# A loop that deals out projections between sine and exponential stages: eleven spends a group with a share for each group, and u's first step placed by group

## The chip, the core and the metric

The kernel runs on one core of one Trainium2 chip. The metric is the device time of one execution in microseconds (us); lower is better. The names of the engines in the profile are PE (TensorE's matmuls), PEld (its weight loads), DVE (VectorE), ACT (ScalarE), POOL (GpSimd) and SP (the queue that issues most DMAs).

## The reference: what is computed

A gated mix of two blocks over one sequence x of 2048 rows and 448 columns (x is `A_u`):

```python
g = _sigmoid((x * gate_w).sum(-1, keepdims=True))
a = _A_ref(x, ...)   # K = 2 Re sum_n C exp(A dt l); y = causal convolution of x with K, by FFT; + x * D_skip
b = _B_ref(x, ...)   # q, k, v = x @ wq, wk, wv; 16 heads of 28; 4 segments of 512 rows:
                     #   causal softmax attention inside a segment, mixed with a memory
                     #   M, z of the segments before (phi(q) M / phi(q) z); then @ wo
return g * a + (1 - g) * b
```

## The kernel before, in words

The work has two halves. The **first half** (`first_half`, L316) computes the convolution kernel K and has the attention's projections dealt out between its steps. The **second half** (`second_half`, L1250) does the Fourier transforms of K and u, the attention, and the output. It starts with `transform_k`, which needs all of K, and with the first loads of q and k. This change touches the first half alone.

*The loop of the first half.* K is made in 56 steps (`n`, L475) of eight channels, four to a group, so 14 groups (`n // 4`). For a step, `turns` (PE) makes the angles of the *next* step, `trig` (L411, ACT) takes three activations for sine and cosine, `product` (L421, DVE, its four instructions at L428 to L436) multiplies them with the exponentials into X and Y, two buffers each, and `sums` (L438, PE) contracts X and Y of the step *before* over the states: 64 small matmuls into `ps_k`. Between two groups stand `decays(g)` (L459): the exponentials of the next group, one ER (`decay_x`, L353) and two EY (`decay_y`, L379). Each has a matmul, then an exponential on ACT; POOL turns them into EX and EH. Since the exponential and the sine are in different tables, ACT loads a table ahead of the decays and one behind them. Inside decays, `sums` of the last step of the group before stand behind the first EY.

*The projections.* `project` (L720) is a generator: it yields the estimated cost of what it has just issued, in us. For each of four segments s of 512 rows it transposes x (four steps of 1.0), makes v (`values`, four tiles of 128 rows, two steps of 1.2 each), and q and k in units (s, hg, m): four heads hg, m = 0 for q and 1 for k. A unit is twelve matmuls (`matmuls`, L782), three to a step of 0.65, with weights that `load_w` fetches from DRAM a unit ahead, into two buffers. The first steps split the weights into two parts each and store them to DRAM (`weights`, L751: eight steps of -0.3 and 0.6, with a copy on ACT, a subtraction on POOL at L766, and a store; their two buffers are those of `load_w`). Most units need an exponential too (phi). They go in pairs, and after a pair the generator yields `"pe"`: the projections are then *held*, with two of the three PSUM buffers `ps_m` in use, until ACT has the table of exponentials. The others (`plain`) need none. A pair that is through leaves its memory to be done (`remember`): for q a recall (1.0), for k a transposition (-1.1) and a memory product (0.6). A negative cost ends the spend that it is in.

*u's first step.* `transform_u` (L552) multiplies u with a Fourier matrix, in 32 halves (16 positions w, two halves each). A half is a load, a matmul into `ps_m`, a copy and a store to GU. With `k.pairs` it does both halves of a w in one step, otherwise one.

*What sets the order.* PE runs in program order. In the loop `k.strict` chains ACT's activations and copies in program order as well. The order is thus what the class `Feed` (L501) deals out: `spend` adds credit to `due` and takes steps of the projections while there is credit and they are not held; `exps` releases a hold just ahead of each of the three exponentials in decays; `rest` does what is left after the loop. In the kernel before, a spend follows each `trig` and each part of decays, seven in a group, `due` is capped at 4.0 and set to zero when a hold is released. u's step is reached in two ways: as a step inside `project` (13 places that yield `-next(filling, 0.1)`, in pairs) and one half at a time when more than 1.5 is due during a hold. With `k.exps` (the second and third spend of decays) copies go to DVE instead of ACT. `feed.fill` does halves of u near the end.

Of the kernel before, what the change touches and what calls it, by code (L numbers as in the profile page):

```python
# [315 lines left out]
def first_half(nc, k, gy, feed):  # L316
# [142 lines left out]
    def decays(g):  # L459
        for i, (f, J) in enumerate(((decay_x, 2 * g), (decay_y, 2 * g), (decay_y, 2 * g + 1))):  # L460
            f(J)
            if g > 0 and i == 1:
                sums(4 * g - 1)
            if g > 0:
                k.exps = i >= 1
                feed.spend(PLACE[i] * RATES[g])
                k.exps = False

    room = []
# [5 lines left out]
    for n in range(2 * NJ):  # L475
        if n < 4:
            load(n + 2)
        elif n % 2 == 0:
            load(n // 2 + 4)
        if n % 4 < 3:  # L480
            turns(n + 1)
        trig(n)
        feed.spend(1.87 * RATES[n // 4])
        product(n)
        if n == 2 * NJ - 1:
            feed.fill(2)
        if n % 4 > 0:
            sums(n - 1)
        if n % 4 == 3 and n + 1 < 2 * NJ:
            decays(n // 4 + 1)  # L490
            turns(n + 1)
# [1 line left out]
    sums(2 * NJ - 1)  # L493


PLACE = (1.24, 0.9, 0.9)

RATES = (1.65, 1.65, 1.24, 1.55, 1.55, 1.17, 1.17, 1.48, 1.55, 1.17, 1.17, 1.48, 1.48, 1.65)


class Feed:  # L501
# [5 lines left out]
    def __init__(self, k, steps, filling):  # L507
        self.k = k
        self.steps, self.held, self.done, self.due, self.count = steps, False, False, 0.0, 0
        self.filling, self.waiting, self.ends = filling, False, False  # L510

    def step(self):
        tag = next(self.steps, None)
# [3 lines left out]
        self.ends = cost < 0  # L517
        return abs(cost)

    def spend(self, us):  # L520
        self.due = min(self.due + us, 4.0)
        self.ends = False
        while self.due > 0 and not (self.held or self.done or self.ends and self.waiting):
            self.due -= self.step()
        if self.due > 1.5 and (self.held or self.done) and self.waiting:
            self.k.pairs = False
            self.due -= next(self.filling, 0.0)
            self.k.pairs = True

    def exps(self):  # L530
        if self.held:
            self.due = 0.0
            self.step()

    def until(self, n):
# [181 lines left out]

def project(nc, k, pp, early, filling):  # L720

    act, copy, v = k.act, k.copy, nc.vector
    gw = pp.tile([112, 4, 2], F32, name="gw")
# [161 lines left out]

    for s in range(NSEG):
        if s > 0:
            yield -next(filling, 0.1)
        xh = pp.tile([112, 4, SEG], F32R, tag="xh", name="xh")
        xl = pp.tile([112, 4, SEG], F32R, tag="xl", name="xl")  # L890
        for t in range(4):
            xin = pp.tile([128, D], F32, tag="xin", name="xin", bufs=4)
            with k.issue_after(holds[s]) if s in holds else ExitStack():
                nc.sync.dma_start(xin, k.u[SEG * s + 128 * t : SEG * s + 128 * t + 128])
            pt = k.ps("m")
            for kt in range(4):
                k.tr(
                    pt[:112, 128 * kt : 128 * kt + 128], xin[:, 112 * kt : 112 * kt + 112], k.ident
                )
            pv = pt[:112].rearrange("p (k q) -> p k q", k=4)  # L900
            ts_ = slice(128 * t, 128 * t + 128)
            copy(xh[:, :, ts_], pv, AF.Copy)
            v.tensor_tensor(xl[:, :, ts_], pv, xh[:, :, ts_], ALU.subtract)
            yield -1.0 if s == 0 or t % 2 else 1.0
        yield from remember()
        if s > 0:
            yield from values(s, xh, xl, range(1))
        if s == 0:
            split = weights()
            for _ in range(4):  # L910
                yield next(split)

        if s == 0:
            plain = [(s, h, 0) for h in range(4)]
            units = [(s, h, 1) for h in range(4)]
        elif s == 3:
            plain = [(s, h, 1) for h in range(4)]
            units = [(s, h, 0) for h in range(4)]
        else:
            plain = []  # L920
# [12 lines left out]
        if s == 0:  # L933
            yield from values(s, xh, xl, range(4))
            for x_ in split:
                yield -0.3
                k.turn_over(k.ps("m"), 3)
                yield 0.6
            yield from rest_of(plain)
        for i in range(0, len(units), 2):  # L940
            us = units[i : i + 2]
            pts = []
            light = i == 2 if s == 0 else i > 2 and s < 3
            if s > 0 and i == 2:
                yield from values(s, xh, xl, range(1, 4))
                store_v(s)
            for u in us:
                if pts:
                    for _ in range(1 if light else 0):
                        yield -next(filling, 0.1)  # L950
                    yield from remember()
                    for _ in range(1 if light else 0):
                        yield -next(filling, 0.1)
                pts.append((yield from matmuls(u, x)))
                load_w(after[u])
                yield 0.65
            yield "pe"
            es, his, phs = [], [], []
            for u, pt in zip(us, pts):
                es.append(raised(pt))  # L960
                his.append(high(u, pt))
            for u, pt, e, hi in zip(us, pts, es, his):
                phs.append(phi(pt, e))
                store(u, pt, hi)
            if s == 0 and i == 0:
                store_v(s)
            pending += zip(us, phs)
            yield 0.1
        if s == 3:
            yield from rest_of(plain)  # L970
# [399 lines left out]
def gated_mix(ctx, tc, k):  # L1370
    nc = tc.nc
# [17 lines left out]
        return tc.keep_in_program_order(nc.scalar.activation(*args, **kw))  # L1389

    k.exps = False
    k.pairs = True

    def copy(out, x, f, **kw):

# [144 lines left out]
    with ExitStack() as st:  # L1540
# [17 lines left out]
        pp = pool(st, "pp", "right")  # L1558
        tu = transform_u(nc, k, pool(st, "up", "right"))

        def work(proj):
            for i, tag in enumerate(proj):
                yield tag
                if i == 100:
                    more_constants()

        gy = pool(st, "gy", "right")
        with ExitStack() as s2:
            early, prm = pool(s2, "early"), pool(s2, "prm", "right")
            feed = Feed(k, work(project(nc, k, pp, prm, tu)), tu)  # L1570
            half = first_half(nc, k, gy, feed)
            load_decay, load_phase, decays, room = next(half)
            params = prepare_params(nc, k, prm, early, gp)
            n = next(params)
            k.ct = gp.tile([128, 2, 512], BF16, name="ct")
            constants()
            while n is not None:
# [10 lines left out]
                n = next(params, None)  # L1588
# [68 lines left out]
```

## Time and profile before

| | |
|---|---|
| runs of the kernel, us | 897.26, 907.48, 912.32 (median 907.48) |
| the profiled execution, us | 906.73 |
| its span in the trace, us | 904.3 |
| mean granted clock of TensorE | 0.92 |
| the loop's groups 0 to 13, us from the span's start | 66.6 to 424.6 |
| last sums end, first transform of K starts | 430.4, 476.4 |

The span runs from the first to the last instruction. Busy time of an engine counts its instructions, not its queue. Matmuls are pipelined, so the mean duration of one is longer than the distance from one to the next; the time of a block of matmuls is read from its first start to its last end. In the timeline and the chain the columns are start, duration, engine, line, what it writes and reads, how many, and in brackets the idle time before it with what ended it. In the busy time by stretches a row has the stretch, its length, the busy time of each engine, the mean granted clock, the share of the DMA engines and their rate.

### The profile page before, as it was taken

To read this page: it belongs to the slowest core of one execution; us is meant where nothing else is said; L and a number is where in the kernel's file an instruction comes from. 1 tells how busy PE (TensorE), PEld (TensorE's weight loads), DVE (VectorE), ACT (ScalarE), POOL (GpSimd) and SP (SyncE) were. 2 spreads that over 40 slices of the span, in tenths; PEclk is the share of its full clock that TensorE was granted. 3 is DMA by queue.
4 is the path that set the end of the run, shared out by engine and by line. 5 is a ranking of instruction groups with operands and counts; after the bars stand their busy time and mean duration, and the time that the engine had idled before them with its cause. 6 is when DMAs were issued, how large, how long until landed. Compare 5 with 4: busy or idle time off the path is not lost.

```text
span 904.3 us, 19003 instructions
## 1 busy us (share of the span) xinstructions
PE 761.0 (84%) x7549; PEld 418.0 (46%) x7549; DVE 609.0 (67%) x1151; ACT 501.5 (55%) x609; POOL 243.8 (27%) x301
## 2 busy tenths in 40 slices
PE   1686798888889788977987799989997999788997
PEld 1363455646446455644763344434443444334433
DVE  7888468778688878989425655656475646765564
ACT  4857477788878888787322135545354434342320
POOL 5234333034333333332000011132222122333110
PEclk9998899999889998998997759999999999988799
DMA  9236664133246312442377775665566465455773
GB/s 229 81 86 189 187 212 151 42 106 132 75 162 211 133 62 93 150 157 80 124 267 280 266 271 156 198 233 192 190 198 199 156 231 189 151 178 206 200 241 100
DMA packets 88290, 152.91 MB, mean 169 GB/s; under 512 B 20626, under 2 KB 57290, under 8 KB 88154
## 3 DMA queue, kind: packets, MB, share of 16 engines
q1 hardware_dynamic: 79130, 140.64, 48.1%
q10 hardware_dynamic: 7424, 9.18, 2.9%
q0 software_dynamic: 1648, 1.89, 0.7%
q8 instruction: 59, 0.97, 0.5%
q14 instruction: 29, 0.24, 0.1%
HBM read 90.67 MB, written 60.63 MB: 167 GB/s over the span
## 4 chain that ended last, share of the span: by engine, by line
PE 52%; DVE 16%; ACT 14%; DMA 8%; issue 6%; SPq 2%; POOL 1%; ACTq 0%; DVEq 0%; POOLq 0%
PE ps_a L1416 19%; PE ps_m L1416 18%; PE ps_pv L1416 7%; ACT cs L1380 7%; PE ps_arg L1416 4%; PE ps_k L1416 3%; DVE jk L1037 3%; DVE Y L434 2%; DVE X L428 1%; ACT L1380 1%; PE ps_m L1419 1%; DMA ku<-KD 1%; DMA w<-WD 1%; DMA WD<-wsp 1%; DVE Y L435 1%
## 5 line engine op out<-in xcount | busy, mean ns | idle before, releaser
L1037 DVE CUSTOM_DVE_ANT_0 jk<-ps_a,mk 128x512 f32<-128x512 f32 (+3 forms) x256 | 125.0, 488 | 54.5 <-PE ps_a L1416 47.2
L1068 ACT ACTIVATE PT<-ps_a 128x1024 f32<-128x1024 f32 (+1 forms) x96 | 84.5, 881 | 124.4 <-PE ps_a L1416 107.5
L1380 ACT ACTIVATE cs<-ps_arg 128x1024 f32<-128x1024 f32 x111 | 107.4, 1022 | 17.8 <-PE ps_arg L1416 15.7
L1416 PE MATMUL ps_m<-xh,w 112*128 112x512 f32 x256 | 91.6, 413 | 11.8 <-DMA w<-WD 10.3
L1416 PE MATMUL ps_k<-Y,X 128*32 128x64 f32 x3584 | 69.4, 235 | 32.7 <-DVE Y L435 31.0
L1079 POOL TENSOR_SCALAR_AFFINE_SELECT PT<-PT 128x256 f32<-128x256 f32 (+1 forms) x96 | 47.4, 496 | 181.1 <-ACT PT L1068 176.7
L1416 PE MATMUL ps_a<-qu,ku 32*128 32x512 f32 (+3 forms) x768 | 92.8, 363 | 1.3 <-DVE mx L1037 0.6
L376 POOL TENSOR_TENSOR EX<-ER,cab 128x512 f32<-128x512 f32 x28 | 29.9, 1089 | 217.7 <-ACT ER L1380 206.6
L1416 PEld LDWEIGHTS ps_k<-Y,X 128*32 128x32 f32 x3584 | 59.0, 119 | 58.9 <-DVE Y L435 44.8
L428 DVE TENSOR_TENSOR X<-EX,cs 128x1024 f32<-128x1024 f32 x56 | 71.4, 1275 | 18.9 <-ACT cs L1380 17.1
L434 DVE TENSOR_TENSOR Y<-EY,cs 128x1024 f32<-128x1024 f32 x56 | 72.5, 1294 | 0.0
L1416 PEld LDWEIGHTS ps_a<-qu,ku 32*128 32x128 f32 x768 | 64.6, 200 | 10.1 <-issue 3.2
L390 POOL TENSOR_TENSOR EH<-EY,ga 128x512 f32<-128x512 f32 x56 | 66.4, 1213 | 5.6 <-ACT EY L1389 4.9
L1416 PE MATMUL ps_a<-ku,qu 32*128 32x512 f32 (+3 forms) x256 | 48.6, 419 | 18.9 <-DMA ku<-KD 10.2
L1416 PEld LDWEIGHTS ps_m<-xh,w 112*128 112x128 f32 x256 | 49.0, 191 | 31.5 <-issue 15.7
L436 DVE SCALAR_TENSOR_TENSOR Y<-EH,cs 128x512 f32<-128x512 f32 x56 | 43.8, 783 | 28.0 <-ACT cs L1380 23.1
L1380 ACT ACTIVATE cs<-cs 128x1024 f32<-128x1024 f32 x56 | 59.3, 1059 | 1.8
L1416 PEld LDWEIGHTS ps_a<-ku,qu 32*128 32x128 f32 x256 | 23.7, 201 | 67.8 <-issue 34.3
L1416 PE MATMUL ps_arg<-ct,lh 64*128 64x512 bf16 x224 | 45.6, 409 | 7.7 <-ACT cs L1380 5.9
L1416 PE MATMUL ps_m<-xl,w 112*128 112x512 f32 x128 | 50.8, 397 | 0.0
L646 DVE TENSOR_TENSOR pr<-ps_a,ks 128x896 f32<-128x896 f32 x32 | 34.7, 1085 | 15.8 <-PE ps_a L1416 15.4
L1416 PE MATMUL ps_m<-wo,pvs 128*128 128x448 f32 x96 | 42.6, 590 | 1.6 <-ACT tb L1172 1.4
(221 smaller groups left out, 1437.0 us busy)
## 6 DMA issues: line engine op xcount, KB each, us to landing
w<-WD SPq DMA_DIRECT2D x32, 448.0 KB
qu<-QD SPq DMA_DIRECT2D x16, 512.0 KB
ku<-KD SPq DMA_DIRECT2D x16, 512.0 KB
GU<-gs SPq DMA_DIRECT2D x32, 224.0 KB
GK<-gs SPq DMA_DIRECT2D x8, 896.0 KB
gk<-GK SPq DMA_DIRECT2D x32, 224.0 KB
gu<-GU SPq DMA_DIRECT2D x32, 224.0 KB
BB<-bs ACTq DMA_DIRECT2D x16, 448.0 KB
```

What stands on the lines that cost most here:

```text
L376: nc.gpsimd.tensor_tensor(o[:, :, :, :16], r, over(k.cab, lo, hi, 16), ALU.mult)
L390: nc.gpsimd.tensor_tensor(EH[J, c].rearrange("p t (d l) -> p t d l", l=32), EY[J][:, c].rearrange("p t (d l) -> p t d l", l=32), over(k.ga ...
L428: v.tensor_tensor(X, ex, t[:, :, 0], ALU.mult)
L434: v.tensor_tensor(Y[:, :, :, :32], lo, y[:, :, :, ::-1], ALU.mult)
L435: v.tensor_tensor(Y[:, 0, :, 32:], hi, y[:, 0], ALU.mult)
L436: v.scalar_tensor_tensor(Y[:, 1, :, 32:], hi, -1.0, y[:, 1], ALU.mult, ALU.mult)
L646: nc.vector.tensor_tensor(pr[c], pt, ks.pop(c), ALU.mult)
L1037: v.tensor_tensor_reduce(junk[:, :n], pt[:, x, o : o + n], k.mk[:, SEG - n :], 1.0, -3e38, ALU.add, ALU.max, mx[:, 3 - t, h : h + 1],)
L1068: nc.scalar.activation(PT[:, 2 * hp : 2 * hp + 2, 512 * b : 512 * b + n], pt[:, :, :n], AF.Exp, scale=SCALE)
L1079: nc.gpsimd.affine_select(sl, sl, pat, ALU.is_ge, 0.0, base=0, channel_multiplier=-1)
L1380: x = op(*args, **kw)
L1416: tc.keep_in_program_order(nc.tensor.matmul(*args, **kw))
```

## The change

Four things, all in how work is dealt out; nothing that is computed changes.

1. A spend names its group and a slot. There are eleven in a group: three in decays (0.9, 0.7, 0.7) and two for each step, one behind `trig` and one behind `sums` (0.5 each). Each gives its part, slot / 6.3, of the group's share in `SHARES`.
2. `due` has no cap any more and isn't set to zero when a hold is released.
3. u's first step leaves `project` and the holds. Each group has a number in `FILLERS`, dealt out over the same slots; when a whole one has come together, both halves of a w are done, whether or not the projections are held. They sum to 13 of the 16 w; the last three are halves at the end (two, four, and two in `rest`).
4. `k.pairs` is false outside of that.

```diff
-                feed.spend(PLACE[i] * RATES[g])
+                feed.spend(g, PLACE[i])
...
         trig(n)
-        feed.spend(1.87 * RATES[n // 4])
+        feed.spend(n // 4, TRIG)
         product(n)
         if n == 2 * NJ - 1:
             feed.fill(2)
         if n % 4 > 0:
             sums(n - 1)
+        feed.spend(n // 4, TRIG)
...
-PLACE = (1.24, 0.9, 0.9)
-RATES = (1.65, 1.65, 1.24, 1.55, 1.55, 1.17, 1.17, 1.48, 1.55, 1.17, 1.17, 1.48, 1.48, 1.65)
+PLACE = (0.9, 0.7, 0.7)
+TRIG = 0.5
+SHARES = (12.4, 11.6, 8.9, 15.2, 15.3, 8.1, 8.1, 14.5, 15.3, 8.1, 8.1, 14.5, 14.6, 12.8)
+FILLERS = (1, 0, 2, 0, 0, 2, 3, 0, 0, 2, 3, 0, 0, 0)
+SLOTS = sum(PLACE) + 8 * TRIG
...
-    def spend(self, us):
-        self.due = min(self.due + us, 4.0)
+    def spend(self, g, share):
+        part = share / SLOTS
+        self.due += SHARES[g] * part
+        self.credit += FILLERS[g] * part
         self.ends = False
         while self.due > 0 and not (self.held or self.done or self.ends and self.waiting):
             self.due -= self.step()
-        if self.due > 1.5 and (self.held or self.done) and self.waiting:
+        if self.credit > 0.99:
+            self.credit -= 1.0
+            self.k.pairs = True
+            next(self.filling, None)
             self.k.pairs = False
-            self.due -= next(self.filling, 0.0)
-            self.k.pairs = True
 
     def exps(self):
         if self.held:
-            self.due = 0.0
             self.step()
...
-            yield -next(filling, 0.1)
+            yield -0.1
...
-                    for _ in range(1 if light else 0):
-                        yield -next(filling, 0.1)
                     yield from remember()
-                    for _ in range(1 if light else 0):
-                        yield -next(filling, 0.1)
```

More of the change, by code (lines that the diff above doesn't have):

```diff
@@ L509, in __init__ @@
         self.steps, self.held, self.done, self.due, self.count = steps, False, False, 0.0, 0
-        self.filling, self.waiting, self.ends = filling, False, False
+        self.filling, self.waiting, self.ends, self.credit = filling, False, False, 0.0
     def step(self):
@@ L716, in finish, with project @@
     return load, join, last
-def project(nc, k, pp, early, filling):
+def project(nc, k, pp, early):
     act, copy, v = k.act, k.copy, nc.vector
@@ L942, in project @@
             pts = []
-            light = i == 2 if s == 0 else i > 2 and s < 3
             if s > 0 and i == 2:
@@ L1391, in gated_mix @@
     k.exps = False
-    k.pairs = True
+    k.pairs = False
     def copy(out, x, f, **kw):
@@ L1569, in gated_mix @@
             early, prm = pool(s2, "early"), pool(s2, "prm", "right")
-            feed = Feed(k, work(project(nc, k, pp, prm, tu)), tu)
+            feed = Feed(k, work(project(nc, k, pp, prm)), tu)
             half = first_half(nc, k, gy, feed)
```

## The prediction

> **What bounds the kernel now.** I began with the totals of the page, then took the busy time by stretches, with the cuts at the loads of the exponential table on ScalarE, which open each group of the loop.
>
> ```profile
> span 904.3 us, 19003 instructions
> PE 761.0 (84%) x7549; PEld 418.0 (46%) x7549; DVE 609.0 (67%) x1151; ACT 501.5 (55%) x609; POOL 243.8 (27%) x301
> ```
>
> ```profile
> core 0: us, PE busy (x) PEld busy (x) DVE busy (x) ACT busy (x) POOL busy (x), PEclk, DMA share, GB/s
> 66.60:123.80 57.20, 42.49 (x607) 25.72 (x603) 37.23 (x39) 33.31 (x38) 20.54 (x17) 0.88 0.64 193
> 123.80:224.60 100.80, 86.81 (x1386) 54.48 (x1386) 78.30 (x100) 84.77 (x101) 35.60 (x32) 0.95 0.39 123
> 224.60:424.60 200.00, 169.52 (x2656) 104.35 (x2656) 163.93 (x208) 163.87 (x187) 70.46 (x64) 0.93 0.37 124
> 424.60:430.40 5.80, 3.83 (x129) 3.43 (x129) 5.80 (x10) 3.45 (x6) 0.52 (x1) 0.50 0.25 93
> 430.40:476.40 46.00, 41.31 (x190) 32.11 (x186) 15.52 (x29) 14.21 (x25) 1.60 (x1) 0.99 0.57 194
> ```
>
> The rows are groups 0 and 1, groups 2 to 5, groups 6 to 13, the last sums, and then 46.0 us in which PE is busy 41.31 and DVE and ACT 15: the projections that the loop left over. In the loop no engine is full: of the middle 100.80 us PE has 86.81, ACT 84.77, DVE 78.30. The chain of waits through the leftover runs on PE, and on loads of weights:
>
> ```profile
> 436.00 23.75 PE ps_m L1416 x108
> 459.77 3.48 DMA w<-WD
> 463.38 3.02 PE ps_m L1416 x12
> 466.42 5.14 DMA w<-WD
> 479.67 6.50 DMA ku<-KD
> ```
>
> 108 matmuls in 23.75 us are nine blocks of twelve at 2.64 us: that is a projection unit (q or k of four heads) or 128 rows of v. A quarter unit is 0.66.
>
> **The deal, worked out from the code.** Each step of the projections names a cost, and a spend takes steps until its credit is used. Adding these costs gives the order of both kernels. Before, the loop ends as (2,3,k) is held: all of segment 3 (32 quarter units, 8 half rows of v, the transposes, five recalls) is left. After, the shares use up everything but the gates and two halves of u. So the 46.0 us go, and their work must fit into the loop.
>
> The holds do not all fall where the shares mean them to. Groups 0 and 1 deal out 12.4 x 4/6.3 + 11.6 = 19.47. From the point where the parameters are done, the first hold is 21.8 away (weights 6.0, four plain units at 2.65, two held units at 2.6). The missing 2.3 are dealt in the three spends of decays(2), and the hold comes after that group's last exponential. So it stays until decays(3). The next two come late likewise, the uncapped due climbs to 13.2 at the end of group 3 and 13.4 at the end of group 4, and is worked off in two bursts: in group 4's second turn (memory, v rows, two units), and in decays(5), first spend (three blocks of v rows, a unit, a recall, a transpose). From group 6 on each hold falls in the decays as meant.
>
> **The parts and their prices.** The small steps, from PE's timeline:
>
> ```profile
> 131.13 0.91 PE L1416 MATMUL ps_m<-ut,s1u 64*128 64x448 f32 x2
> 430.37 2.03 PE L1419 MATMUL ps_m<-ident,xin 128*112 128x128 f32 x12
> 433.70 1.12 PE L1416 MATMUL ps_m<-ph,macc 128*128 128x512 f32 x2
> 434.67 0.60 PE L1419 MATMUL ps_m<-ident,ph 128*128 128x128 f32 x4
> 436.00 1.16 PE L1416 MATMUL ps_m<-v,pkT 128*128 128x128 f32 x8 [0.74 <-ACT pkT L1380]
> ```
>
> In that order: a half of u's step, three input transposes (0.68 each), a recall, a key transpose, a memory product.
>
> (1) The tail: -46.0. What comes in its place is two halves of u after the last sums, 2 x 0.91, and up to 2 us of waits for their copies. The four halves before the last sums lie beside DVE, which is busy for all of 424.60 to 430.40. I take +3 (ends +2 and +4). The load of ku (6.50) stands behind the last stores in SP's queue, before (AM, DM) as after (GU): no change.
>
> (2) Groups 0 and 1. Eight spends instead of four bring the last six weight splits forward, two a turn. The chain there now:
>
> ```profile
> 73.42 5.40 DMA WD<-wsp
> 82.96 1.71 POOL wsp L766
> 84.68 3.39 DMA WD<-wsp
> 89.83 3.22 DMA WD<-wsp
> 93.12 3.61 DMA w<-WD
> 96.87 4.62 PE ps_m L1416 x12
> ```
>
> There are two buffers, so a pair of splits costs about 1.7 on POOL and 3.2 to 5.4 for the store, and the third pair waits on ACT ahead of the turn after it. Pairs at 70, 78 and 84 us end the stores near 89.5, and the first unit starts near 93, not 96.87. But PE now meets it in turn 3, ahead of the sums and of decays(1), which were beside the wait before. From there two quarter units, the sums and decays of 9 to 11 us (8.9 in the rows of part 3) move trig 4 from 102.50 (its row is there too) to about 107. Group 1's four turns then carry 12 quarter units, not 20 (7.7 us of PE, where 13.2 were): about 15 us instead of 21.3. Sum -1; from -6 to +8, if either half alone holds.
>
> (3) Groups 2 to 5. What decays cost today, on ScalarE:
>
> ```profile
> 102.50 1.02 ACT L1380 ACTIVATE cs<-ps_arg 128x1024 f32<-128x1024 f32 x1 [11.04 <-PE ps_arg L1416]
> ...
> 276.15 1.28 ACT L1380 ACT_TABLE_LOAD   x1
> ...
> 282.68 1.02 ACT L1380 ACTIVATE EY<-ps_arg 128x1024 f32<-128x1024 f32 x1 [1.26 <-PE ps_arg L1416]
> 283.72 1.28 ACT L1380 ACT_TABLE_LOAD   x1
> 285.09 1.94 ACT L1380 ACTIVATE cs<-ps_arg 128x1024 f32<-128x1024 f32 x2
> ```
>
> That is 8.9 us, and each EY waits for its matmul, which stands behind the spend ahead of it on PE. In decays(5) that spend is now 4 x 2.64 + 1.12 + 0.60 = 12.3 us. Then come the sums, a memory product, a unit and a pair of u's halves while two of three PSUM buffers are held, so that its second half waits for a copy: 1.1 (the 64 sums, below) + 1.16 + 2.64 + 1.82 + 0.6 for the wait = 7.3. With the last EY (1.02), the table (1.28) and the waits around them decays(5) take about 24 us: +15. Group 4: the burst of 1.16 + 3 x 2.64 = 9.1 stands before the sums that free X and Y, of which there are two: about +5; its decays get the four input transposes that group 3 had, +4.5. Groups 2 and 3 have nearly idle turns: -1 and -4. Sum +19. At best the bursts pay for themselves in part beside DVE and ACT: +8; at worst the work added here, 10 us of PE, comes on top: +28.
>
> (4) Groups 6 to 13 take in 22 quarter units, 8 half rows of v, 4 transposes and 4 recalls more, and one memory product and 4 halves of u (with the two behind the last turn) fewer: 14.5 + 10.6 + 2.7 + 4.5 - 1.2 - 3.6 = 27 us of PE. What that costs, from groups 4 to 11:
>
> ```profile
> 177.80:200.20 22.40, 18.83 (x322) 10.35 (x322) 13.13 (x15) 19.14 (x22) 8.57 (x8) 0.92 0.31 96
> 200.20:224.50 24.30, 21.79 (x350) 14.86 (x350) 19.88 (x27) 21.66 (x26) 9.58 (x8) 1.00 0.40 138
> 224.50:248.00 23.50, 19.29 (x324) 11.04 (x324) 16.52 (x20) 19.21 (x23) 8.63 (x8) 0.85 0.23 72
> 248.00:276.10 28.10, 24.88 (x320) 13.91 (x324) 22.09 (x29) 21.28 (x25) 8.57 (x8) 0.88 0.46 148
> 276.10:299.10 23.00, 21.11 (x319) 12.55 (x307) 20.94 (x28) 21.31 (x26) 8.62 (x8) 1.00 0.66 217
> 299.10:328.70 29.60, 23.91 (x423) 16.45 (x424) 25.64 (x36) 22.21 (x27) 8.17 (x8) 0.94 0.28 93
> 328.70:350.90 22.20, 17.89 (x316) 9.79 (x316) 15.67 (x17) 19.12 (x21) 9.56 (x8) 0.85 0.23 77
> 350.90:375.00 24.10, 23.07 (x299) 16.29 (x300) 20.04 (x27) 21.32 (x26) 9.57 (x8) 1.00 0.37 132
> ```
>
> The three sparse groups (4, 6, 10) take 22.7 us with 18.7 of PE. The two that were dealt evenly (8, 11) take 23.55 with 22.1: 0.25 us for each us of work. All five dense ones take 25.8 with 22.95: 0.73. Smaller spends speak for the first; the waits that stay (transposes and memory products between PE and a copy) for the second. I take 0.5: +13.5; ends 0.25 (+7) and one for one (+27).
>
> (5) Queues. u's loads and stores on SP are as many as before, moved by some groups; a GU store holds SP until its copy, at most about 3 us, with a weight load behind it, and that load is a unit ahead. Without that cover it is 3.61. POOL's splits move ahead of EX and EH, which wait for ER anyway. Both at nothing.
>
> Sum: -46 + 3 - 1 + 19 + 13.5 = -11.5. The profiled execution took 906.73 us, so 895.2; the median of the three runs, 907.48, stands 0.75 above it: 896.
>
> **The rivals.** *The loop soaks it up.* At 0.25 in (4) and the lower end in (3): -46 + 3 - 1 + 8 + 7 = -29, 878 us. For it speak groups 8 and 11; against it, that the due is 13 when group 5 begins. Or my count to the first hold is wrong, the shares do what they say, and (3) is near zero: 877.
>
> *PE becomes the bound.* Every moved us of PE costs one, in groups 2 to 5 too: -46 + 3 - 1 + 29 + 27 = +12, 919 us, slower than now. Its place is every group from 4 on; with (3) at +19 it turns the sign once a us of work costs more than 0.93. For it: group 9, 29.60 us with 23.91 of PE. Against it: group 11, 24.10 with 23.07.
>
> *A denser loop runs at a higher clock.* The granted clock is 0.88 to 0.95 in the loop's rows and 0.99 in the tail, and one and the same set of 64 sums has taken
>
> ```profile
> 138.08 1.93 PE L1416 MATMUL ps_k<-Y,X 128*32 128x64 f32 x64 [2.52 <-DVE Y L435]
> ...
> 143.09 1.10 PE L1416 MATMUL ps_k<-Y,X 128*32 128x64 f32 x64
> ```
>
> At full clock PE's busy time in the three loop rows would shrink by 42.49 x 0.12 + 86.81 x 0.05 + 169.52 x 0.07 = 21 us at most; at 0.5 us for each, -10.5, 886 us. Against it: group 4 and 5 get long waits in which PE has nothing. By the Trainium skill (TensorE: Matmul & The Clock Gate, Part 1: The HAM clock gate) an idle window of some 3.4 us puts PE at half rate and as much steady work brings it back. By that rule, the trace agrees as far as the slow set stands behind a gap of 2.52 us; the even groups would gain and the held ones lose.
>
> **How the numbers follow.** About 2% (18 us) is what a measurement of this kernel can tell from no change: below 889.3 is faster, above 925.6 slower. The forecast has 0.55 (0.01 of it below 889.3); the loop that soaks it up, with the shares in place, 0.22; the clock 0.05; PE as the bound 0.18, of which 0.11 goes past 925.6, since the start's +8 would come on top. Faster 0.28, same 0.61, slower 0.11. The corners of the sum are 872 and 928; 8 times in 10 I expect 876 to 919; the forecast's own range is 888 to 907.
>
> **What would show it.** The leftover stretch between the last sums and the first transform of k falls from 46 to under 6 us. Trig 4 starts near 107 us. Decays(5) are the longest, about 24 us between two table loads and their trig, with ACT waiting for PE before an EY for some 8 us. Groups 6 to 13 take about 213 us together. I am wrong if decays(5) are like the others, or if groups 6 to 13 stay near 200 or pass 225, or if new waits in the second half turn up.

## The result, and the profile after

The changed kernel takes 934.33 us (median of 4 runs, 930.52 to 940.81) where the kernel before took 903.52 beside it (4 runs, 897.26 to 912.32). The ratio is 1.037, with a 95% interval of 1.027 to 1.048: slower by some 31 us. The forecast was 896, within 876 to 919, so the time moved the other way and past the range. The profiled execution took 930.52 us at a mean granted clock of 0.912 (before 906.73 at 0.920).

The first fence has the totals of the page after, the second its busy time by stretches. The stretches are groups 0 and 1, groups 2 to 5, groups 6 to 13 (these three cut at the table loads, as in the prediction), the last sums, the leftover, the first transform of K, and the rest.

```profile
span 928.8 us, 18972 instructions
PE 766.4 (83%) x7528; PEld 415.5 (45%) x7549; DVE 606.7 (65%) x1155; ACT 499.3 (54%) x605; POOL 241.0 (26%) x301
```

```profile
core 0: us, PE busy (x) PEld busy (x) DVE busy (x) ACT busy (x) POOL busy (x), PEclk, DMA share, GB/s
65.70:124.50 58.80, 40.24 (x598) 23.73 (x597) 35.92 (x38) 33.52 (x38) 20.86 (x17) 0.85 0.62 184
124.50:261.40 136.90, 107.85 (x1440) 70.23 (x1441) 84.22 (x116) 85.63 (x100) 32.74 (x32) 0.84 0.32 103
261.40:505.60 244.20, 206.86 (x2841) 126.09 (x2841) 174.28 (x228) 174.42 (x208) 68.93 (x64) 0.93 0.39 127
505.60:510.30 4.70, 4.70 (x75) 2.15 (x75) 3.50 (x4) 2.36 (x6) 0.53 (x1) 1.00 0.80 277
510.30:514.70 4.40, 1.38 (x8) 0.54 (x8) 2.28 (x9) 2.41 (x5) 1.59 (x1) 0.88 0.50 183
514.70:542.00 27.30, 25.16 (x150) 11.11 (x150) 17.61 (x44) 7.61 (x9) 0.61 (x1) 0.83 0.88 321
542.00:928.80 386.80, 346.99 (x2303) 158.72 (x2319) 235.84 (x640) 152.63 (x188) 88.52 (x151) 0.93 0.62 200
```

Against the rows of before: the leftover falls from 46.00 to 4.40 us, groups 0 and 1 from 57.20 to 58.80, but groups 2 to 5 grow from 100.80 to 136.90 and groups 6 to 13 from 200.00 to 244.20. The loop pays 80 us for a tail of 42. Over all rows the two profiled spans lie 24.5 us apart, less than the medians' 31: the profiled execution after is the shortest of its four. Some executions of a kernel are slower than its others; the medians below are over all of them, the ratios leave the slow ones out, and of e14, whose profile is of a slow one, only the times are used.

The same span once more, cut at the end of the last `trig` of group 1, of group 5 and of the loop (the cut that I use for every version below), first before, then after:

```profile
118.70:224.10 105.40, 90.62 (x1462) 57.20 (x1461) 80.76 (x103) 84.31 (x101) 35.60 (x32) 0.95 0.39 125
224.10:424.60 200.50, 169.91 (x2665) 104.45 (x2660) 164.43 (x208) 164.34 (x188) 70.46 (x64) 0.93 0.37 124
```

```profile
120.90:258.80 137.90, 108.47 (x1442) 70.38 (x1441) 85.22 (x117) 85.57 (x99) 32.74 (x32) 0.84 0.33 107
258.80:505.60 246.80, 209.28 (x2912) 127.80 (x2912) 176.88 (x232) 174.48 (x209) 68.93 (x64) 0.93 0.38 126
```

Read the lengths against PE's busy time. Groups 2 to 13 take 384.7 us instead of 305.9: +78.8. PE is busy 317.75 us instead of 260.53: +57.2. So PE stands without work for 67.0 us instead of 45.4: +21.6. The deal, worked out from the code with the prediction's durations, puts 167.8 us of PE into these groups where 132.4 were: +35.4. The three parts of the growth are thus 35.4 of work (an estimate from durations of the kernel before), 21.8 by which PE is busy beyond it, and 21.6 of more waiting. The forecast had assumed that the waiting would shrink.

**A late hold, from the inside.** Group 2 after, by halves:

```profile
114.00:134.00 20.00, 17.60 (x298) 10.41 (x287) 13.33 (x16) 12.10 (x13) 7.02 (x7) 1.00 0.54 161
134.00:152.30 18.30, 11.05 (x148) 5.52 (x147) 10.91 (x12) 12.33 (x14) 1.11 (x2) 0.52 0.25 81
```

The hold comes in decays(2), and from 134 us on the projections are held for the rest of the group. PE has turns, sums and one pair of u left, waits for the products, and its granted clock falls to 0.52. In PE's timeline, one half of u (two matmuls) before that stretch, and the sums and one half of the pair in it:

```profile
126.29 1.10 PE L1420 MATMUL ps_k<-Y,X 128*32 128x64 f32 x64
...
128.21 1.02 PE L1420 MATMUL ps_m<-ut,s1u 64*128 64x448 f32 x2
...
139.69 1.93 PE L1420 MATMUL ps_k<-Y,X 128*32 128x64 f32 x64 [2.20 <-DVE Y L435]
141.55 1.86 PE L1420 MATMUL ps_m<-ut,s1u 64*128 64x448 f32 x2
...
147.54 1.93 PE L1420 MATMUL ps_k<-Y,X 128*32 128x64 f32 x64
```

64 sums take 1.93 us here and 1.10 before it; two matmuls of u 1.86, and 1.02 some thirteen microseconds earlier. ScalarE stands behind them, because its instructions are chained in program order and u's copies (`gs`) come ahead of the next `trig`:

```profile
138.50 1.06 ACT L1384 ACTIVATE cs<-cs 128x1024 f32<-128x1024 f32 x1
143.45 0.54 ACT L1384 ACTIVATE gs<-ps_m 128x448 f32<-128x448 f32 x1 [3.90 <-PE ps_m L1420]
145.94 0.54 ACT L1384 ACTIVATE gs<-ps_m 128x448 f32<-128x448 f32 x1 [1.95 <-PE ps_arg L1420]
146.38 1.93 ACT L1384 ACTIVATE cs<-ps_arg 128x1024 f32<-128x1024 f32 x2
```

So this group, with hardly any projections, is not a quick one: 5.85 us of ScalarE's time go by in these waits.

**The burst**, ScalarE in decays(5), from one table load to the next and the `trig` behind it:

```profile
214.04 1.28 ACT L1384 ACT_TABLE_LOAD   x1
...
227.97 0.60 ACT L1384 ACTIVATE am<-ps_m 128x512 f32<-128x512 f32 x1 [3.06 <-PE ps_m L1420]
...
228.94 1.03 ACT L1384 ACTIVATE EY<-ps_arg 128x1024 f32<-128x1024 f32 x1
234.01 0.60 ACT L1384 ACTIVATE e<-ps_m 128x512 f32<-128x512 f32 x1 [4.04 <-DMA AM<-am]
...
238.34 1.02 ACT L1384 ACTIVATE EY<-ps_arg 128x1024 f32<-128x1024 f32 x1 [2.17 <-PE ps_arg L1420]
239.38 1.28 ACT L1384 ACT_TABLE_LOAD   x1
242.96 1.94 ACT L1384 ACTIVATE cs<-ps_arg 128x1024 f32<-128x1024 f32 x2 [2.30 <-PE ps_arg L1420]
```

These are the blocks that the deal had placed there: three of v's rows, a unit, a recall and a transposition ahead of the first EY, then the next hold's exponentials (`e`) ahead of the second. 28.9 us lie between the table load at 214.04 and the `trig` at 242.96. The wait at 234.01 is for a store: in `project` the recall's copy `am` and the exponential's `e` share one tag of two buffers, and the unit that the first `e` reads had ended by 227.1. The chain, and PE at u's second half, show what hangs on it:

```profile
229.14 4.80 DMA AM<-am
...
238.24 2.86 PE ps_m L1420 x6
```

```profile
236.52 0.64 PE L1420 MATMUL ps_m<-ut,s1u 64*128 64x448 f32 x1 [2.01 <-DVE lo L816]
```

`e` waits for that store, DVE's `lo` stands behind `e`, u's second half waits for the buffer that `lo` frees, and the second EY's matmul stands behind u on PE. Behind that EY come the six matmuls of the third spend and the angles, for which the `trig` waits 2.30 us.

### The profile page after: what moved, and what is told of

It is laid out like the page before. It is cut to its first block, busy times and chain, and to the rows that moved or that the text cites. A ratio compares the mean times of both kernels' runs of the same rounds, so it can differ in the third digit from the quotient of the medians.

```text
span 928.8 us, 18972 instructions
## 1 busy us (share of the span) xinstructions
PE 766.4 (83%) x7528; PEld 415.5 (45%) x7549; DVE 606.7 (65%) x1155; ACT 499.3 (54%) x605; POOL 241.0 (26%) x301
## 4 chain that ended last, share of the span: by engine, by line
PE 48%; DVE 17%; ACT 12%; DMA 11%; issue 8%; POOL 3%; SPq 1%; ACTq 0%; DVEq 0%; POOLq 0%
PE ps_m L1420 16%; PE ps_a L1420 16%; PE ps_pv L1420 6%; ACT cs L1384 6%; PE ps_k L1420 4%; PE ps_arg L1420 3%; DVE jk L1041 3%; DVE Y L434 2%; PE ps_m L1423 2%; DVE X L428 2%; DMA w<-WD 2%; DMA RD<-rs 2%; DMA WD<-wsp 1%; DVE Y L435 1%; DVE e L830 1%
## 5 line engine op out<-in xcount | busy, mean ns | idle before, releaser
L1420 PE MATMUL ps_m<-xh,w 112*128 112x512 f32 x256 | 101.5, 437 | 14.9 <-DMA w<-WD 14.9
L428 DVE TENSOR_TENSOR X<-EX,cs 128x1024 f32<-128x1024 f32 x56 | 68.4, 1222 | 39.4 <-ACT cs L1384 27.6
L436 DVE SCALAR_TENSOR_TENSOR Y<-EH,cs 128x512 f32<-128x512 f32 x56 | 39.0, 698 | 50.6 <-ACT cs L1384 33.3
L434 DVE TENSOR_TENSOR Y<-EY,cs 128x1024 f32<-128x1024 f32 x56 | 70.1, 1252 | 0.0
L390 POOL TENSOR_TENSOR EH<-EY,ga 128x512 f32<-128x512 f32 x56 | 60.6, 1107 | 25.3 <-ACT EY L1384 20.3
L1420 PE MATMUL ps_arg<-ct,lh 64*128 64x512 bf16 x224 | 49.4, 418 | 4.5 <-ACT cs L1384 3.4
```

The lines of the kernel that those rows point to most:

```text
L390: nc.gpsimd.tensor_tensor(EH[J, c].rearrange("p t (d l) -> p t d l", l=32), EY[J][:, c].rearrange("p t (d l) -> p t d l", l=32), over(k.ga ...
L428: v.tensor_tensor(X, ex, t[:, :, 0], ALU.mult)
L434: v.tensor_tensor(Y[:, :, :, :32], lo, y[:, :, :, ::-1], ALU.mult)
L436: v.scalar_tensor_tensor(Y[:, 1, :, 32:], hi, -1.0, y[:, 1], ALU.mult, ALU.mult)
L1420: tc.keep_in_program_order(nc.tensor.matmul(*args, **kw))
```

## The experiments

Sixteen kernels ran, in four sets, each set beside the kernel before on one chip, whose median was 906.16, 905.58, 904.42 and 904.06 us; each ratio is to the kernel before of its set. Differences across sets are of medians on different chips, so a few microseconds of them say nothing. I had three theories of the loss. AMOUNT: the loop cannot take in the leftover's work at all. PLACE and HOLDS: it can, but not where the change puts it (the spend behind the sums; the late first hold). U: the difference is made by where u's halves go.

**First set: the place of the second spend, the first hold, both, and the amount alone.** Each edit is against the changed kernel, but for the fourth, which is the kernel before with one line changed.

```diff
# e1: the second spend ahead of the sums
         product(n)
...
+        feed.spend(n // 4, TRIG)
         if n % 4 > 0:
             sums(n - 1)
-        feed.spend(n // 4, TRIG)
# e2: a larger first share, so that the first hold comes at the end of group 1
-SHARES = (12.4, 11.6, ...
+SHARES = (16.2, 11.6, ...
# e3: both
# e4: the kernel before, rates times 1.2
+RATES = tuple(1.2 * r for r in (1.65, 1.65, 1.24, ...
```

> The changed kernel with the second spend of each step moved ahead of the sums of the step before; the deal (which step in which slot) stays the same. Theory PLACE: behind the sums, a step whose result ScalarE copies puts that copy ahead of the next trig, and PE reaches it only after the sums, which wait for DVE's product; so each such step ties the next trig to the product before. Then groups 6 to 13 (244 us now, 200 before) fall to 210 to 225 and the time to 900 to 915. Theory AMOUNT: the loop pays for the PE work that was moved into it, wherever it stands: no change, 930 to 938. Groups 2 to 5 keep most of their 137 us by both.

> The changed kernel with the first group's share 16.2 instead of 12.4, so that every hold is reached at the end of its group and released at the first exponential of the next. Theory HOLDS: the late first hold, with its backlog and two bursts, costs what groups 2 to 5 lost: they fall from 137 us to 100 to 112, the time to 900 to 912. If the backlog was harmless and the amount counts, the work is only moved between groups: time 930 to 938, groups 6 to 13 up or down by what groups 2 to 5 give.

> Both edits: second spend ahead of the sums and first share 16.2. PLACE and HOLDS together: groups 2 to 5 near 105, groups 6 to 13 near 215, time 870 to 885. AMOUNT: 925 to 938.

> The kernel before with all its rates times 1.2 and nothing else: by the costs in the code this deals out all projections in the loop, in the old seven spends a group, with the old cap and the old halves of u. AMOUNT: the loop grows as in the changed kernel, 244 us for groups 6 to 13, and the time is 925 to 938. PLACE: the tail of 46 us goes and the loop grows by about half of it; time 878 to 890.

| | us (median) | ratio to before, 95% |
|---|---|---|
| e1, spend ahead of the sums | 915.46 | 1.016, 1.009 to 1.023 |
| e2, first share 16.2 | 913.30 | 1.008, 1.003 to 1.013 |
| e3, both | 914.17 | 1.010, 1.001 to 1.020 |
| e4, the rule of before, all dealt out | 883.19 | 0.979, 0.973 to 0.986 |

AMOUNT falls: e4 has the same leftover dealt out in the loop and is 2% faster than before, within PLACE's range. Late holds are worth 21 us (e2), and the spend behind the sums 19 (e1), both a little less than PLACE and HOLDS had said; e3 lies in neither of its ranges. PE's longest group of waits, the sums' for the product, over groups 2 to 13 of the kernel after and of e1:

```profile
PE ps_k L1420 <- DVE Y L435: 33.1, 18, 3.2
```

```profile
PE ps_k L1420 <- DVE Y L435: 16.3, 11, 3.0
```

The second spend, put ahead of the sums, is done while they would wait: 33.1 us become 16.3. But the two gains do not add up. e3 is no better than either. Its loop is as long as theirs (359.7 us from the end of group 1, against 358.4 and 359.3). In e3 this wait is 22.1 us, and ScalarE's wait ahead of EY is the longest of the three (20.2 in e1, 32.8 in e2):

```profile
ACT EY L1384 <- PE ps_arg L1420: 53.3, 16, 8.9
```

So what the sums wait less, ScalarE waits more in the decays. The deal of e2 and e3 is the same, so why these waits grow stays open, and that they are what eats the second gain is a reading that no run isolates.

**Second set: lighter decays, the reset of `due`, a higher rate.** e5 and e7 start from e3, e6 from e2 (the second spend behind the sums), e8 from before.

```diff
# e5 and e6
-PLACE = (0.9, 0.7, 0.7)
+PLACE = (0.3, 0.2, 0.2)
-TRIG = 0.5
+TRIG = 0.7
-SHARES = (16.2, 11.6, ...
+SHARES = (11.6, 11.6, ...
# e7
         if self.held:
+            self.due = 0.0
             self.step()
# e8: the kernel before, rates times 1.3
```

> The kernel of both edits (holds in place, second spend ahead of the sums) with the slots of the decays cut from 0.9, 0.7, 0.7 to 0.3, 0.2, 0.2 and those of the steps raised from 0.5 to 0.7 (first share 11.6, so that the first hold stays in place): by the costs in the code PE's work dealt into the decays of groups 2 to 13 falls from 70 to 41 us and that of the turns rises from 96 to 125. Theory COVER: only work between a trig and the sums behind it lies beside DVE's product; in the decays it is on the path. Then PE's stretches of the decays (144 us in the kernel of both edits, 102 in the kernel with rates times 1.2) fall to 95 to 110, the turns grow by no more than 25, and the time is 878 to 895. Rival U: what made the kernel with rates times 1.2 fast is u's halves in the holds, and shifting the rest changes nothing: 905 to 915.

> The same light decays with the second spend behind the sums, as the change has it. COVER: the work behind the sums does not cover the wait for the product, so PE's wait at the sums is 10 us or more longer than with the spend ahead, and the time 10 to 20 us above that kernel. If only the decays mattered: within 5 us of it.

> The kernel of both edits with the due set to zero again when a hold is released, as before the change. By the costs in the code the decays' work falls from 70 to 61 us, the amount that the kernel with rates times 1.2 has there, and all holds fall in the last spend of a group. COVER: decays 110 to 130 us, time 892 to 905. If it is the carried-over due alone that made the decays long: near 102 us there and 880 to 890.

> The kernel before with rates times 1.3 instead of 1.2: everything is dealt out in the loop with more to spare, holds fall a spend earlier in three groups. Expected 878 to 890 by every theory; below 880 would say that an even earlier deal pays, above 890 that the margin is small.

| | us (median) | ratio to before, 95% |
|---|---|---|
| e5, light decays, second spend ahead | 906.55 | 1.000, 0.995 to 1.004 |
| e6, light decays, second spend behind | 891.46 | 0.985, 0.978 to 0.992 |
| e7, reset | 914.48 | 1.010, 1.003 to 1.018 |
| e8, the rule of before, times 1.3 | 878.24 | 0.970, 0.963 to 0.977 |

Taking work out of the decays (the first share is lowered with it, to keep the first hold in place) gains 22 us from e2 to e6 and 8 from e3 to e5. The place of the second spend now counts the other way: e6, behind the sums, is 15 us faster than e5, where e1 had gained 19 by moving it ahead. The expectation of e6 was wrong in sign, and that of e7 altogether: the reset is worth nothing here. e5 missed COVER's range and lies in that of its rival, U; e8 is at the fast end of its own. The same cut of groups 2 to 13 for e2, e6 and e8:

```profile
123.30:240.00 116.70, 97.82 (x1441) 63.61 (x1439) 87.18 (x122) 83.54 (x96) 32.82 (x32) 0.96 0.37 119
240.00:482.60 242.60, 204.36 (x2903) 126.86 (x2904) 175.32 (x238) 172.07 (x203) 69.31 (x64) 0.93 0.40 131
```

```profile
125.10:237.00 111.90, 96.35 (x1443) 63.72 (x1441) 86.01 (x115) 86.89 (x103) 35.28 (x32) 0.97 0.40 129
237.00:463.70 226.70, 197.68 (x2908) 126.18 (x2908) 167.85 (x228) 176.87 (x213) 67.11 (x64) 0.95 0.42 139
```

```profile
119.40:237.10 117.70, 104.37 (x1394) 66.89 (x1393) 87.62 (x118) 85.75 (x102) 33.76 (x32) 0.93 0.43 137
237.10:453.00 215.90, 193.78 (x2933) 125.72 (x2936) 177.74 (x238) 172.55 (x204) 68.81 (x64) 0.98 0.46 150
```

From 384.7 us after, e2 comes to 359.3 (its gain lies in groups 2 to 5, 137.9 to 116.7), e6 to 338.6 (now groups 6 to 13, 242.6 to 226.7) and e8 to 333.6, with PE busy 317.8, 302.2, 294.0 and 298.2.

**Third set: one spend or two, u dealt as before or by group.** e9 is e4 with u's pairs placed by group as in the change; e10 is e6 with one spend of 1.4 behind `trig`; e12 is e6 with u's halves as steps of the projections and one at a time during holds; e11 is both edits.

```diff
# e9, on e4
+        self.credit += FILLERS[g] * slot / SLOTS
...
-        if self.due > 1.5 and (self.held or self.done) and self.waiting:
-            self.k.pairs = False
-            self.due -= next(self.filling, 0.0)
+        if self.credit > 0.99:
+            self.credit -= 1.0
             self.k.pairs = True
+            next(self.filling, None)
+            self.k.pairs = False
# e10, on e6
-        feed.spend(n // 4, TRIG)
         if n % 4 == 3 and n + 1 < 2 * NJ:
...
-TRIG = 0.7
+TRIG = 1.4
# e12, on e6: the reverse of the diff of e9, and
+SHARES = (11.6, 11.6, 12.5, 15.2, 15.3, 11.7, 13.5, 14.5, 15.3, 11.7, 13.5, 14.5, 14.6, 12.8)
```

> The kernel before with rates times 1.2 (883 us) and one part of the change alone: u's first step placed by group in pairs, out of the projections and out of the holds. By the deal worked out from the code the projections' share of decays stays (62.1 us of PE for 61.0), the turns lose u's halves (104.4 for 113.1), eight halves are left for the end instead of none to speak of (+4 us there), and four pairs fall into holds. Theory U (u's halves in the holds fill PE's waits, and a pair that falls into a hold or beside a whole unit is paid for in full): 892 to 905. Theory S (the second spend of a step and the uncapped due are what the rest costs, u's place is worth nothing): 883 to 888, the longer end alone.

> The kernel after with light decays (slots 0.3, 0.2, 0.2), the first share of 11.6, and one spend a step of 1.4 behind trig instead of 0.7 there and 0.7 behind the sums (891 us with two). The deal is the same group by group. Theory S: the spend behind the sums puts copies ahead of the next trig on ScalarE and delays it, so one spend gives 876 to 884. Theory U: 888 to 895, no difference. A third way: blocks of twice the size make the product wait for PE's sums, 895 to 905.

> The kernel after with light decays, one spend a step, and u's halves dealt as in the kernel before (as steps of the projections, and one at a time in a hold with more than 1.5 due), the shares raised by 1.8 for each w that a group had. What is left of the change is the uncapped due and a share for each group. Theory U: 875 to 884. Theory S: 876 to 884 too, the same as with one spend alone. If both are worth something the gains add up to 868 to 875, which would beat every version so far.

> The kernel after with light decays, both spends of a step, and u's halves dealt as in the kernel before, the shares raised by 1.8 for each w that a group had. The only thing that differs from the version with light decays behind the sums (891 us) is u's place. Theory U: 875 to 884. Theory S: 887 to 894.

| | us (median) | ratio to before, 95% |
|---|---|---|
| e9, rule of before, u by group | 898.03 | 0.993, 0.989 to 0.996 |
| e10, one spend, u by group | 885.95 | 0.982, 0.978 to 0.987 |
| e11, one spend, u as before | 887.35 | 0.982, 0.977 to 0.987 |
| e12, two spends, u as before | 903.12 | 0.997, 0.994 to 1.001 |

One spend a step is better than two by 16 us from e12 to e11. From e6 to e10 it is 5.5 us, and the intervals overlap (0.978 to 0.992, 0.978 to 0.987); in the profiles all of that lies in the start, where group 2 begins at 119.3 us instead of 125.1. For u's place there is no such answer: by group it costs 15 us (e4 to e9), nothing (e11 to e10), or gains 12 (e12 to e6). Of the expectations only U's for e9 was met; e10 fell between its two ranges, and e11 and e12 were slower than both of theirs. Both of my theories fail on one of the pairs.

**Fourth set: u's pairs out of the decays, and the price of the decays.**

```diff
# e13, on e9
-        self.credit += FILLERS[g] * slot / SLOTS
+        self.credit += FILLERS[g] / 4 if slot == TRIG else 0.0
# e14, on the changed kernel: the slots alone
-PLACE = (0.9, 0.7, 0.7)
-TRIG = 0.5
+PLACE = (0.3, 0.2, 0.2)
+TRIG = 0.7
# e15, on e10
-PLACE = (0.3, 0.2, 0.2)
-TRIG = 1.4
-SHARES = (11.6, 11.6, ...
+PLACE = (0.9, 0.7, 0.7)
+TRIG = 1.0
+SHARES = (16.2, 11.6, ...
# e16, on e10: the edit of e13
```

> The version of before with rates times 1.2 and u placed by group in pairs (898 us; with u in the holds 883), the pairs now dealt only behind trig, none in the decays. PE's work in the decays of groups 2 to 13 goes from 62.1 to 52.6 us, in the turns from 104.4 to 113.9, and pairs that fall into a hold go from 4 to 11. Theory D (work in the decays costs about 1.5 us a us, in the turns about 0.6): 882 to 891. Theory H (a pair during a hold waits for the one PSUM buffer that is left, and that is what it costs): 900 to 912.

> The kernel after (934 us) with other weights of the slots and nothing else: 0.3, 0.2, 0.2 in the decays and 0.7 in each of the eight others, not 0.9, 0.7, 0.7 and 0.5. By the deal worked out from the code this takes 20 us of PE out of the decays (50.9 for 70.8) and also brings the first holds back to the end of their groups, as the decays no longer overrun them. Theory D with the late holds: both gains come, 892 to 902. If late holds and heavy decays were not the causes, and the second spend or u's place were: 920 to 934.

> The version with one spend a step and light decays (886 us) with the slot weights of the change again (0.9, 0.7, 0.7 in the decays, 1.0 behind each trig) and a first share of 16.2, which keeps the holds at the end of the groups. PE's work in the decays goes from 40.7 to 70.0 us, in the turns from 125.1 to 95.8. Theory D (1.5 against 0.6 for each us): +20 to +30, 903 to 915. If heavy decays hurt only beside the second spend: 884 to 892.

> The version with one spend a step and light decays (886 us), u's pairs dealt only behind trig: decays 31.2 for 40.7 us of PE, turns 134.6 for 125.1, pairs in holds 6 for 1. Theory D: 874 to 882. Theory H: 889 to 897.

| | us (median) | ratio to before, 95% |
|---|---|---|
| e13, rule of before, u's pairs in the turns | 881.52 | 0.976, 0.969 to 0.984 |
| e14, the change with other slot weights | 907.15 | 0.999, 0.994 to 1.005 |
| e15, one spend, heavy decays | 896.60 | 0.988, 0.983 to 0.993 |
| e16, one spend, u's pairs in the turns | 901.39 | 0.998, 0.994 to 1.001 |

e14 says most about the change: two lines of weights, and 27 of its 31 us are gone by the medians, all of them by the ratio (0.999; I had expected 892 to 902 us). It takes work out of the decays and puts the holds in place at once, so it does not tell the two apart. And it differs from e6 in one number alone, a first share of 12.4 instead of 11.6: that costs 1.4% (0.999 against 0.985, and the intervals do not overlap) on the same chip. By the deal those 0.8 us of credit bring some later holds a slot forward and put 10 us more of PE's work into the decays (50.9 for 40.7), so 10 us there go with some 13 us of time.

e15 asks for the price of the decays with holds in place: 29.3 us of PE moved into them cost 10.7 by the medians, half of the least that I had expected and between its two ranges, and about 5 by the ratios, whose intervals overlap. Yet ScalarE's waits ahead of EY (us in total, times, the longest) grow, from e10 to e15, from

```profile
ACT EY L1383 <- PE ps_arg L1419: 28.4, 13, 5.1
```

to

```profile
ACT EY L1383 <- PE ps_arg L1419: 48.2, 17, 8.9
```

e13, at the fast end of D's range, bears out that pairs in the decays cost on the old rule (16.5 us, though more pairs fall into holds), and e16, the same edit on e10, costs 15 us and is slower than both of its ranges. So no fixed price of a slot survives. In e10, where the decays carry little (40.7 us) and the turns much, the pairs were better off in the decays.

**What orders all of them.** PE's time without work in groups 2 to 13 (length less busy time, as above), beside the medians:

| | e4 | e8 | e13 | e11 | e10 | e6 | e5 | e16 | e12 | e9 | e15 | e7 | e3 | e2 | e1 | after |
|---|---|---|---|---|---|---|---|---|---|---|---|---|---|---|---|---|
| PE without work, us | 31 | 35 | 41 | 42 | 44 | 45 | 48 | 49 | 50 | 50 | 51 | 55 | 56 | 57 | 57 | 67 |
| median, us | 883 | 878 | 882 | 887 | 886 | 891 | 907 | 901 | 903 | 898 | 897 | 914 | 914 | 913 | 915 | 934 |

The work dealt out differs by at most 8 us among these sixteen (165.8 to 174.1). The order of the times is nearly that of PE's waiting, and 36 us of waiting go with 51 to 56 us of time. This is a correlation over one profile each, not a cause that an edit isolates. It does not hold to a few microseconds either: e5 waits 3 us less than e15 and is 10 us slower.

## Why the prediction was wrong, step by step

**The tail (step 1)** was right in kind: 46.0 forecast to leave 3 (ends 2 and 4), 46.0 became 4.4. **The start (step 2)** was right, its mechanism too: -1 forecast, +1.6 measured; the last split's store ends at 89.54 us (forecast near 89.5), the first unit starts at 93.92 (near 93), and trig 4 at 107.36 (near 107). Group 1's turns then took 17.2 us where 15 were put down.

```profile
107.36 1.95 ACT L1384 ACTIVATE cs<-ps_arg 128x1024 f32<-128x1024 f32 x2 [0.20 <-PE ps_arg L1420]
```

**Groups 2 to 5 (step 3)** came to +32.5 in the cut above (+36.1 by table loads) where +19 was taken and +28 was the end. The count of the deal was right: the holds come late, decays(5) are the longest by far. Two sizes were wrong. Decays(5) took 28.9 us, not 24. The spend ahead of the first EY was right to a microsecond (13.25 us on PE for 12.3). Between the two EY 7.3 us had been put down, with 0.6 for u's wait; 9.4 passed, and u waited 2.01 at the end of the chain from the store of `am`. The third spend (2.86 us on PE), behind which the `trig` waits 2.30 more, is not named in the sum. And groups 2 and 3, which I had put down as gains of 1 and 4 us because they carry little, took 31.4 and 28.9 us against 28.0 and 26.6:

```profile
120.90:152.30 31.40, 21.95 (x319) 11.36 (x318) 17.34 (x21) 18.25 (x19) 8.13 (x8) 0.72 0.38 121
152.30:181.20 28.90, 22.00 (x344) 15.20 (x344) 19.30 (x27) 20.11 (x23) 8.23 (x8) 0.83 0.24 75
181.20:213.90 32.70, 26.77 (x386) 19.14 (x390) 24.28 (x36) 20.98 (x25) 8.14 (x8) 0.84 0.21 66
213.90:258.80 44.90, 37.75 (x399) 24.69 (x399) 24.30 (x36) 26.23 (x35) 8.24 (x8) 0.92 0.44 148
```

Groups 2 and 3 alone make 10.7 us of this step's miss of 13; group 5 adds 5.6, and group 4 came out 3 us below its part. In groups 2 and 3 two reasons show, and no run separates them: ScalarE's wait behind the pair of u, above, and the clock column (0.72 and 0.83; 0.95 in all of groups 2 to 5 before). By the Trainium skill (TensorE: Matmul & The Clock Gate, Part 1: The HAM clock gate) the throttled clock is the default state and activity releases it. The trace agrees: 0.52 in the half of group 2 in which PE was held, 1.00 in the half before. I had used that rule for a rival in which a denser loop runs faster; the change made part of the loop sparser. For that rival e8 speaks only in part: with all of the work in the loop, groups 6 to 13 run at 0.98 where 0.93 was before, groups 2 to 5 at 0.93 where 0.95 was.

**Groups 6 to 13 (step 4)** is the step that failed most: "I take 0.5: +13.5; ends 0.25 (+7) and one for one (+27)" turned into +46.3 (+44.2 by table loads), or 1.7 us for each us of work. The price was read from groups that the old rule had dealt. There it holds roughly: e8 and e4, with the old rule and all of the work, have 215.9 and 221.3 us in these groups, +15.4 and +20.8. The changed deal is not at that price, and one for one was no upper end. What the price leaves out is where the work stands: with the same shares in groups 6 to 13, the second spend put ahead of the sums brings 246.8 us there to 228.8 (e1), and lighter decays bring 242.6 to 226.7 (e2 to e6). The growth does not follow the work group by group either: group 10, with three pairs of u, grew from 23.7 to 35.0 us, and group 11, which got no more work than before by the deal, still grew from 24.5 to 28.6. Against before the clock is no reason here: it is 0.93 over these groups in both kernels. What a trace can show is a chain in which each engine waits for the next. In group 7 after, ScalarE's `trig` stands behind the copies of a spend:

```profile
298.10 1.94 ACT L1384 ACTIVATE cs<-ps_arg 128x1024 f32<-128x1024 f32 x2
...
303.83 0.60 ACT L1384 ACTIVATE am<-ps_m 128x512 f32<-128x512 f32 x1 [1.36 <-PE ps_m L1420]
305.63 0.60 ACT L1384 ACTIVATE pkT<-ps_m 128x512 f32<-128x512 f32 x1 [1.20 <-PE ps_m L1423]
306.13 1.94 ACT L1384 ACTIVATE cs<-ps_arg 128x1024 f32<-128x1024 f32 x2
```

PE's next transposition waits in turn for the copy before it, its four matmuls take 1.11 us where 0.60 were priced, and the eight of a memory product 1.84 where 1.16 were:

```profile
304.48 1.11 PE L1423 MATMUL ps_m<-ident,ph 128*128 128x128 f32 x4 [0.69 <-ACT am L1384]
...
307.35 1.84 PE L1420 MATMUL ps_m<-v,pkT 128*128 128x128 f32 x8
```

**The queues**: ku's load, whose wait of 6.50 us step 1 had left as it was, is not in the chain of the changed kernel between 509.59 and 523, and the first transform of K takes 27.3 us instead of 34.4. That gain of 7 us was not forecast. In e8 a wait of 6.36 for the same load stands in the chain at 488.55, so I do not claim that the change removes it for good:

```profile
488.55 6.36 DMA ku<-KD
```

The rest of the second half was 386.8 us instead of 393.5; over the versions it lies between 385 and 400, and the 6.7 us are within that.

**The rivals.** "The loop soaks it up" was taken for a property of the loop; e8 and e4 show that it depends on the deal. "PE becomes the bound" had the right sign (919 us), with the wrong cause: PE was without work for 67 us of groups 2 to 13, more than before. The change's plan itself can work: e6 keeps all of it (eleven spends, shares, pairs by group) with other weights and a smaller first share, and is 1.5% faster than before; with the first share of the change (e14) the gain is gone.

**Left open.** Which wait makes up the excess of groups 6 to 13: several edits each take part of it off, and none isolates one wait. Why 0.8 us of the first share cost 1.4% (e6, e14). Why u's place costs on one base and gains on another; why the second spend ahead of the sums gains with the weights of the change and loses with light decays (e1, e5, e6). In each, several waits change at once. The best of these versions is the old rule at 1.3 times the rates, 878.24 us, faster than both kernels, with u's halves still in the holds.

## What to carry to other kernels

A price read from the trace ("half a microsecond for each microsecond of work") belongs to the order in which it was measured; before using it on a new order, ask of each new place which in-order engine stands behind it and whether PE was waiting there. One for one is not the upper end of what inserted work costs. And a stage that loses its filler work need not get shorter by it: here the work that came late was paid for where it piled up (group 5), and groups 2 and 3, where it was missing, grew too.

## What the runs showed of the hardware

The granted clock sank within one group, not only over stages: 1.00 in 114 to 134 us and 0.52 in 134 to 152.3, with PE busy 17.60 of 20.00 and 11.05 of 18.30 us. In the second stretch PE's busy share is 60%; at full clock the same matmuls would fill about 11.05 x 0.52 = 5.7 of the 18.3 us (an estimate from the row, which takes busy time to go with one over the clock, as the sums' 1.10 and 1.93 us nearly do).

The same estimate for the 21.8 us of busy time beyond the work dealt out: in groups 2 to 5 the clock went from 0.95 to 0.84, and at 0.95 their 108.47 us would have been 95.9, so some 12.6 us may be the clock's. In groups 6 to 13 it is 0.93 in both kernels, and the other 9 us are not explained by it.
